# Second product of the seven-product blocks in 256-column matmuls, with shifted stationary operands

## The chip, the cores and the metric

The kernel runs on one core of a Trainium2 chip. The metric is the device time of one execution in microseconds; three runs of a kernel give a median. Each kernel also has one profiled execution, whose trace gives the start and the length of the instructions of each engine: TensorE (PE, with its loads of the stationary operand in a row of their own, PEld), VectorE (DVE), ScalarE (ACT), GpSimd (POOL) and SyncE (SP).

## What is computed

Attention with a memory term over 4 x 8 heads of 576 positions and 64 dimensions, and then two expert layers without biases over 2304 tokens of 512 features with 2048 inner features. Only the expert layers matter here:

```python
def _moe_ref(x, w_in, w_out):
    h = x @ w_in
    g = h * np.cos(h)
    return (g @ w_out).astype(np.float32)

def _moe2_ref(x, w_in, w_out):
    h = x @ w_in
    r = np.maximum(h, 0.0)
    g = r * r
    return (g @ w_out).astype(np.float32)

x = attention(q, k, v, M_prev, z_prev, beta)      # to rows of tokens x 512
return _moe2_ref(_moe_ref(x, w_in, w_out), w2_in, w2_out)
```

## The kernel before

Tokens go through an expert layer in blocks of 512, 512, 512, 256 and 512 (`CFG["sizes"]`), and the 2048 inner features in 16 feature tiles of 128. A *step* s is one feature tile f of one block j in layer p (`steps[s] = (p, j, f)`). For each step TensorE makes the first product h (128 inner features x the block's tokens), the other engines make the activation g from it, and TensorE makes the second product, which adds up over the 16 feature tiles in PSUM.

Products are to be as exact as float32, from operands in the type float32r. So each operand is kept as a high part and a rest (h and l at the end of its name: `winh`, `winl`, `wouth`, `woutl`, `gh`, `gl`), and a product is three matmuls: high x high, high x rest, rest x high. `g_f` (line 373) makes gh on ScalarE and `g_g` (line 379) gl on VectorE or GpSimd. Both take a tile of 128 x 512 from the pool `g3`, which keeps two buffers for each of the two names (line 332).

The second product is `l2` (line 880). In layer 1 the stationary operand is a 128 x 128 piece of wout and the moving one is g. In layer 2 it is the other way around: the stationary operand is a 128 x 128 piece of g, the moving one is all 512 columns of wout, and the result is 128 tokens x 512 outputs, one bank of PSUM (`acc[c]`). `evac` (line 919) copies these banks to SBUF after the last feature tile and starts their way out.

Layer 2 has two ways of making the first product. Its narrow block (256 tokens, `order2`) makes it directly, as layer 1 does (`l1`, line 310). The other four blocks (`CFG["seven"]`, steps from NS = 80 on) use Strassen's scheme with seven products for two feature tiles at a time: `product(k, i)` (line 1168) makes product i of pair k as six matmuls of 256 columns, and `combine` (line 1185) puts the products together on ScalarE and VectorE. The loop over k (line 1239) writes out the order of the work: between the seven products of pair k it puts the second product of the two steps before, in pieces (`l2(s0 - 2)` whole, `l2(s0 - 1)` in two halves of its four output tiles). There are 32 pairs, and so 64 such steps of four output tiles.

Moving operands of 256 columns don't begin at the start of their tile but 48 elements further: `span` (line 307) for the narrow block, `xpart` (line 1119) for the seven products. All others begin at the start.

Of the kernel before, what the change touches and what calls it, by code (L numbers as in the profile page):

```python
# [10 lines left out]
F32R = mybir.dt.float32r  # L11
# [116 lines left out]
def kernel(  # L128
# [39 lines left out]
    pe, act, dve, pool, sync = nc.tensor, nc.scalar, nc.vector, nc.gpsimd, nc.sync  # L168
# [125 lines left out]
    steps = [(p, j, f) for p, j, a, e in segs for f in range(a, e)]  # L294
    NS = len(steps)
    segs7 = [(2, j, 0, NF) for j in CFG["seven"]]
    steps += [(p, j, f) for p, j, a, e in segs7 for f in range(a, e)]
    opens = {(p, j, a) for p, j, a, e in segs + segs7}
    closes = {(p, j, e - 1) for p, j, a, e in segs + segs7}
# [7 lines left out]
    def span(n):  # L307
        return slice(48, 48 + n) if n == 256 else slice(0, n)
# [23 lines left out]
    g_3 = ctx.enter_context(tc.tile_pool(name="g3", bufs=2))  # L332
# [36 lines left out]
    def g_e(s):  # L369
        if steps[s][0] == 1:  # L370
            dve.tensor_tensor(out=rs[s], in0=hs[s], in1=rs[s], op=ALU.mult)

    def g_f(s):
        n = blocks[steps[s][1]][1]
        gh = g_3.tile([128, 512], F32R, tag="gh", name="gh")[:, span(n) if steps[s][0] == 1 else slice(0, n)]
        act.activation(out=gh, in_=rs[s], func=AF.Copy)
        gs[s] = gh

    def g_g(s):
        n = blocks[steps[s][1]][1]  # L380
        gl = g_3.tile([128, 512], F32R, tag="gl", name="gl")[:, span(n) if steps[s][0] == 1 else slice(0, n)]
        eng = pool if s < CFG["glp"] else dve
        eng.tensor_tensor(out=gl, in0=rs[s], in1=gs[s].bitcast(F32), op=ALU.subtract)
        gs[s] = (gs[s], gl)

    chain, made = {"a": g_a, "b": g_b, "c": g_c, "d": g_d, "s": g_s, "e": g_e, "f": g_f, "g": g_g}, set()

    def g_do(x, s):
# [487 lines left out]
    def moe(ctx, g_o, early):  # L876
        ps_a = ctx.enter_context(tc.tile_pool(name="psa", bufs=1, space=PSUM))
        acc, part = {}, {}

        def l2(s, span_=(0, 1)):  # L880
            p, j, f = steps[s]
            n = blocks[j][1]
            hi, lo = wt[p, "out", f]
            gh, gl = gs[s]
            na = KD if p == 1 else n // 128
            for c in range(int(span_[0] * na), int(span_[1] * na)):
                if (p, j, f) in opens:
                    acc[c] = ps_a.tile([128, 512], F32, tag=f"a{c}", name=f"a{c}")
                cs = slice(c * 128, (c + 1) * 128)
                if p == 1:  # L890
                    o = acc[c][:, 0:n]
                    ops = ((hi[:, cs], gh), (hi[:, cs], gl), (lo[:, cs], gh))
                else:
                    o = acc[c]
                    ops = ((gh[:, cs], hi), (gl[:, cs], hi), (gh[:, cs], lo))
                for x, (lt, rt) in enumerate(ops):
                    pe.matmul(
                        out=o, lhsT=lt, rhs=rt,
                        start=((p, j, f) in opens and x == 0),
                        stop=((p, j, f) in closes and x == 2),  # L900
                    )

        def evac_tile(c, s=0):
            if c < 2:
# [78 lines left out]
        def step(name, u, s):  # L983
# [4 lines left out]
            elif name == "L2":  # L988
                if live:
                    l2(u)  # L990
                    l2_done.add(u)
# [247 lines left out]
        for k in range(K):  # L1239
# [28 lines left out]
            if kb == (6 if k < KP else 2) and nx is not None:  # L1268
                for x in ("t1", "t2", "t3"):
                    t_make(nx, x)  # L1270
            l2(s0 - 2)
            if last:
                for x in ("b11", "b21", "t3"):
# [11 lines left out]
            if last:  # L1285
                for x in ("t2", "t4"):
                    x_h(nx, x)
                    x_l(nx, x)
            l2(s0 - 1, (0, .5 if k < K - 1 else .25))
            evac(s0 - 1, (0, .5))  # L1290
            product(k, 5)
# [94 lines left out]
```

## Time and profile before

| | us |
|---|---|
| median of 3 runs | 967.05 (966.15 to 967.24) |
| the profiled execution | 965.75 |
| its span, from the first to the last instruction | 964.0 |
| TensorE busy in the span | 956.0 (99%) |
| VectorE | 663.7 (69%) |
| ScalarE | 568.5 (59%) |

The median is read for the time, and the span for where it goes. The rest of the profiled execution's time, 1.75 us, lies around the span. A matmul's length in the trace reaches into those after it, as they are pipelined; the distance from one start to the next is what one costs when nothing waits. The lines of the trace nearly all show L48, which is the helper that hands out the instructions, so the groups are told apart by the names of their tiles: `a` is the second product's bank, `h` the first product's, `out<-moving,stationary` in either order of names.

### The profile page before, as it was taken

How to read it: one execution, taken by the hardware profiler on the slowest of the kernel's cores; microseconds unless marked ns; L12 is line 12 of the kernel's file. 1: busy time of each engine (PE TensorE's matmuls, PEld its weight loads, DVE VectorE, ACT ScalarE, POOL GpSimd, SP SyncE). 2: the span in 40 equal slices, each digit the busy share in tenths (PEclk: the TensorE clock that was granted, in tenths of full speed). 3: DMA queues.
4: the chain of work that ended last, by engine and by line, in shares of the span. 5: the costliest groups of instructions: out<-in, count | busy, mean ns of one | idle time of the engine just before them, and what ended most of it. 6: DMA issues, size and time to landing. Idle time of an engine off the chain costs nothing.

```text
span 964.0 us, 16498 instructions
## 1 busy us (share of the span) xinstructions
PE 956.0 (99%) x6030; PEld 811.4 (84%) x6030; DVE 663.7 (69%) x1381; ACT 568.5 (59%) x1235; POOL 214.3 (22%) x295
## 2 busy tenths in 40 slices
PE   8999999999999999999999999999999999999998
PEld 5777777788888888888988888999999999999997
DVE  7988888588989766687788986665654455445433
ACT  7999998777777655665777784443432232233222
POOL 7777876301111000010010002242201001000000
PEclk9999999999999999999999999999999999999999
DMA  6355654452433434243454655343441314223221
GB/s 201 125 168 182 207 208 154 150 165 65 133 97 122 136 110 149 76 142 119 134 172 141 210 167 175 111 156 128 143 152 68 99 66 154 99 66 110 91 73 44
DMA packets 69139, 126.91 MB, mean 132 GB/s; under 512 B 7106, under 2 KB 32194, under 8 KB 69058
## 3 DMA queue, kind: packets, MB, share of 16 engines
q1 hardware_dynamic: 68624, 125.44, 39.8%
q8 instruction: 47, 0.77, 0.3%
q10 hardware_dynamic: 434, 0.43, 0.1%
q14 instruction: 34, 0.28, 0.1%
HBM read 93.86 MB, written 31.98 MB: 131 GB/s over the span
## 4 chain that ended last, share of the span: by engine, by line
PE 86%; DVE 6%; ACT 3%; DMA 2%; issue 2%; SPq 0%; POOL 0%; DVEq 0%; POOLq 0%; ACTq 0%
PE a L48 35%; PE h L48 34%; PE o L48 6%; PE sps L48 5%; PE ptps L48 5%; DVE gf L48 2%; PE qps L48 2%; DVE wa L48 1%; ACT gh L48 1%; DMA wf<-ws2out 1%; DVE wb L48 1%; ACT gf L48 1%; DVE woutl L48 0%; DMA wraw<-in_moe_w_out_dram 0%; DMA qk<-in_qk_dram 0%
## 5 line engine op out<-in xcount | busy, mean ns | idle before, releaser
L48 PE MATMUL h<-xb,winh 128*128 128x256 f32 (+1 forms) x1216 | 289.7, 325 | 0.2 <-DVE gf L48 0.2
L48 PEld LDWEIGHTS h<-xb,winh 128*128 128x128 f32 x1216 | 206.9, 188 | 22.9 <-DVE gf L48 0.4
L48 PE MATMUL h<-xb,winl 128*128 128x256 f32 (+1 forms) x640 | 207.8, 325 | 0.0
L48 PEld LDWEIGHTS h<-xb,winl 128*128 128x128 f32 x640 | 121.7, 190 | 10.0
L48 PE MATMUL a<-gl,wouth 128*128 128x512 f32 (+1 forms) x320 | 118.0, 369 | 0.3 <-DVE gl L48 0.2
L48 PE MATMUL a<-gh,woutl 128*128 128x512 f32 (+1 forms) x320 | 117.6, 367 | 0.0
L48 PE MATMUL a<-gh,wouth 128*128 128x512 f32 (+1 forms) x319 | 117.3, 368 | 0.0
L48 POOL TENSOR_SCALAR wa<-wa 128x512 f32<-128x512 f32 x63 | 39.6, 629 | 343.7 <-ACT wa L48 318.2
L48 PE MATMUL a<-wouth,gl 128*128 128x512 f32 x288 | 112.5, 391 | 0.6 <-DVE gl L48 0.6
L48 PE MATMUL a<-woutl,gh 128*128 128x512 f32 x288 | 112.2, 390 | 0.0
L48 PE MATMUL a<-wouth,gh 128*128 128x512 f32 x288 | 112.2, 390 | 0.0
L48 DVE TENSOR_TENSOR hb<-h,p 128x256 f32<-128x256 f32 x64 | 27.2, 425 | 117.3 <-PE h L48 117.3
L48 POOL TENSOR_SCALAR P<-P,sm 128x384 f32<-128x384 f32 (+3 forms) x128 | 86.4, 691 | 29.3 <-ACT x L48 20.2
L48 PE MATMUL h<-xb,r 128*128 128x256 f32 x576 | 83.7, 282 | 0.0
L48 DVE TENSOR_TENSOR gf<-h,gf 128x512 f32<-128x512 f32 (+1 forms) x80 | 50.7, 634 | 47.9 <-ACT ki L48 41.2
L48 PEld LDWEIGHTS h<-xb,r 128*128 128x128 f32 x576 | 79.2, 189 | 5.3 <-DVE hb L48 0.5
L48 ACT ACTIVATE ki<-h 128x512 int32<-128x512 f32 (+1 forms) x80 | 44.1, 552 | 65.2 <-PE h L48 64.9
L48 ACT ACTIVATE gh<-hb 128x512 fp32r<-128x512 f32 x32 | 20.2, 632 | 92.6 <-DVE hb L48 92.6
L48 ACT ACTIVATE P<-P,mx 128x384 f32<-128x384 f32 (+3 forms) x128 | 70.5, 562 | 2.2 <-DVE mx L45 2.2
L48 ACT ACTIVATE gh<-gf 128x512 fp32r<-128x512 f32 (+1 forms) x96 | 53.4, 556 | 29.2 <-DVE gf L48 28.9
L48 PEld LDWEIGHTS a<-gl,wouth 128*128 128x128 f32 x320 | 60.1, 188 | 10.8 <-DVE gl L48 0.8
L48 PEld LDWEIGHTS a<-gh,woutl 128*128 128x128 f32 x320 | 60.2, 188 | 10.0
(122 smaller groups left out, 1793.5 us busy)
## 6 DMA issues: line engine op xcount, KB each, us to landing
wraw<-in_moe_w_in_dram SPq DMA_DIRECT2D x32, 512.0 KB, 4.0
wraw<-in_moe_w_out_dram SPq DMA_DIRECT2D x32, 512.0 KB, 3.9
r<-sw SPq DMA_DIRECT2D x24, 512.0 KB, 3.5
qk<-in_qk_dram SPq DMA_DIRECT2D x15, 640.0 KB, 5.2
wf<-ws2in SPq DMA_DIRECT2D x32, 256.0 KB, 2.7
r<-sw SPq DMA_DIRECT2D x24, 256.0 KB, 3.7
vr<-in_vrow_dram SPq DMA_DIRECT2D x16, 320.0 KB, 5.3
xT<-x SPq DMA_DIRECT2D x16, 288.0 KB, 2.3
```

The source lines that it names most:

```text
L48: made = call(*args, **kwargs)
```

## The change

In the steps of the seven-product blocks `l2` makes each of its three matmuls on an output tile as two, of columns 0 to 255 and 256 to 511 of wout and of the bank, with the same stationary operand. Only the first half's first matmul opens the bank. The tiles of gh and gl become 528 elements wide, in all steps, and in the steps of the seven-product blocks g stands in elements 16 to 527 of its tile, 64 bytes further than before. In all other steps g stands where it stood within its tile.

```diff
+    def part(s, n):
+        if steps[s][0] == 1:
+            return span(n)
+        return slice(0, n) if s < NS else slice(16, 16 + n)
+
     def g_f(s):
         n = blocks[steps[s][1]][1]
-        gh = g_3.tile([128, 512], F32R, tag="gh", name="gh")[:, span(n) if steps[s][0] == 1 else slice(0, n)]
+        gh = g_3.tile([128, 528], F32R, tag="gh", name="gh")[:, part(s, n)]
         act.activation(out=gh, in_=rs[s], func=AF.Copy)
         gs[s] = gh

     def g_g(s):
         n = blocks[steps[s][1]][1]
-        gl = g_3.tile([128, 512], F32R, tag="gl", name="gl")[:, span(n) if steps[s][0] == 1 else slice(0, n)]
+        gl = g_3.tile([128, 528], F32R, tag="gl", name="gl")[:, part(s, n)]
         eng = pool if s < CFG["glp"] else dve
         eng.tensor_tensor(out=gl, in0=rs[s], in1=gs[s].bitcast(F32), op=ALU.subtract)
         gs[s] = (gs[s], gl)
...
                 else:
                     o = acc[c]
                     ops = ((gh[:, cs], hi), (gl[:, cs], hi), (gh[:, cs], lo))
+                halves = (slice(0, 256), slice(256, 512)) if p == 2 and s >= NS else (slice(None),)
                 for x, (lt, rt) in enumerate(ops):
-                    pe.matmul(
-                        out=o, lhsT=lt, rhs=rt,
-                        start=((p, j, f) in opens and x == 0),
-                        stop=((p, j, f) in closes and x == 2),
-                    )
+                    for hc in halves:
+                        pe.matmul(
+                            out=o[:, hc], lhsT=lt, rhs=rt[:, hc],
+                            start=((p, j, f) in opens and x == 0 and hc.start in (0, None)),
+                            stop=((p, j, f) in closes and x == 2),
+                            skip_group_check=len(halves) > 1,
+                        )
```

## Rows read from the trace of the kernel before

**Rows 1.** The page: busy us, share of the span and instructions, by engine.

```profile
PE 956.0 (99%) x6030; PEld 811.4 (84%) x6030; DVE 663.7 (69%) x1381; ACT 568.5 (59%) x1235; POOL 214.3 (22%) x295
```

**Rows 2.** The page: the chain that ended last, shares by engine and line.

```profile
PE 86%; DVE 6%; ACT 3%; DMA 2%; issue 2%; SPq 0%; POOL 0%; DVEq 0%; POOLq 0%; ACTq 0%
PE a L48 35%; PE h L48 34%; PE o L48 6%; PE sps L48 5%; PE ptps L48 5%; DVE gf L48 2%; PE qps L48 2%; DVE wa L48 1%; ACT gh L48 1%; DMA wf<-ws2out 1%; DVE wb L48 1%; ACT gf L48 1%; DVE woutl L48 0%; DMA wraw<-in_moe_w_out_dram 0%; DMA qk<-in_qk_dram 0%
```

**Rows 3.** Timeline, 631.3 to 634.3: start, length, engine, instruction, count, idle before.

```profile
631.39 0.77 PEld L48 LDWEIGHTS h<-xb,r 128*128 128x128 f32 x6 [0.26 <-DVE hb L48]
631.39 0.97 PE L48 MATMUL h<-xb,r 128*128 128x256 f32 x6
...
632.20 0.39 PE L48 MATMUL h<-xb,winh 128*128 128x256 f32 x2
...
634.24 0.39 PE L48 MATMUL a<-wouth,gh 128*128 128x512 f32 x1
```

**Rows 4.** Timeline of the end: TensorE's last matmul and the copy behind it.

```profile
960.02 0.39 PE L48 MATMUL a<-woutl,gh 128*128 128x512 f32 x1
960.45 0.76 DVE L48 COPY ob<-a 128x256 f32<-128x256 f32 x2 [2.05 <-PE a L48]
```

**Rows 5.** Stretch 634.0 to 960.5: length, engines' busy us, clock, DMA share, GB/s.

```profile
634.00:960.50 326.50, 326.18 (x2056) 295.39 (x2054) 157.99 (x267) 102.92 (x234) 34.55 (x34) 1.00 0.30 102
```

**Rows 6.** TensorE's waits from 635 to the end: us, times, longest.

```profile
PE a L48 <- DVE gl L48: 0.2, 1, 0.2
```

**Rows 7.** TensorE's groups and one load group from 634.2: count, busy, mean ns, idle.

```profile
L48 PE MATMUL a<-wouth,gl 128*128 128x512 f32 x256 | 99.9, 390 | 0.2 <-DVE gl L48 0.2
L48 PE MATMUL a<-woutl,gh 128*128 128x512 f32 x256 | 99.8, 390 | 0.0
L48 PE MATMUL a<-wouth,gh 128*128 128x512 f32 x256 | 99.7, 390 | 0.0
L48 PE MATMUL h<-xb,winh 128*128 128x256 f32 x488 | 90.4, 282 | 0.0
L48 PE MATMUL h<-xb,r 128*128 128x256 f32 x554 | 80.5, 282 | 0.0
L48 PE MATMUL h<-xb,winl 128*128 128x256 f32 x244 | 68.7, 282 | 0.0
...
L48 PEld LDWEIGHTS a<-woutl,gh 128*128 128x128 f32 x256 | 48.1, 188 | 9.9
```

**Rows 8.** The page's costliest groups: matmuls and loads of one operand pair.

```profile
L48 PE MATMUL h<-xb,winh 128*128 128x256 f32 (+1 forms) x1216 | 289.7, 325 | 0.2 <-DVE gf L48 0.2
L48 PEld LDWEIGHTS h<-xb,winh 128*128 128x128 f32 x1216 | 206.9, 188 | 22.9 <-DVE gf L48 0.4
```

**Rows 9.** Timeline of TensorE in the last stage: twelve wide matmuls, twelve narrow ones.

```profile
644.64 0.39 PE L48 MATMUL a<-wouth,gh 128*128 128x512 f32 x1
...
647.36 0.87 PE L48 MATMUL h<-xb,r 128*128 128x256 f32 x6
...
648.77 0.39 PE L48 MATMUL a<-wouth,gh 128*128 128x512 f32 x1
```

**Rows 10.** Timeline of TensorE in layer 1's narrow block, 256 columns throughout.

```profile
464.02 0.38 PE L48 MATMUL a<-gl,wouth 128*128 128x256 f32 x1
464.24 0.29 PE L48 MATMUL a<-gh,woutl 128*128 128x256 f32 x1
...
465.46 0.50 PE L48 MATMUL h<-xb,winh 128*128 128x256 f32 x2
...
466.98 0.28 PE L48 MATMUL a<-gh,wouth 128*128 128x256 f32 x1
...
475.46 0.28 PE L48 MATMUL a<-gh,wouth 128*128 128x256 f32 x1
...
478.40 0.28 PE L48 MATMUL a<-gh,wouth 128*128 128x256 f32 x1
...
486.56 0.28 PE L48 MATMUL a<-gh,wouth 128*128 128x256 f32 x1
```

## The prediction

> **What bounds the kernel now.** I read the busy table first: TensorE works 99% of the span, VectorE 69%, ScalarE 59% [rows 1]. That share alone proves little, so I read the chain of waits next: 86% of it is TensorE, and the two matrix products of the expert layers make up 69% [rows 2]. The change touches the last stage, in which the seven-product blocks run. Its first second-product matmul starts at 634.24 [rows 3] and its last matmul at 960.02 [rows 4]. In that window VectorE is busy for 158.0 and ScalarE for 102.9 of 326.5 us [rows 5], and the list of TensorE's waits holds a single one, 0.2 us, on the way to the last block [rows 6]. So here the time is the number of matmuls times the distance from one start to the next, and nothing else ends later. The granted clock is 1.00 throughout [rows 5], the upper of its two levels. What the change is worth is therefore read from starts, and not from the durations of single matmuls (390 and 282 ns, [rows 7]), which overlap.
>
> **What the change replaces.** In the list of groups the second product of the stage has 256 matmuls for each of three operand pairs, 768 in all, each of 512 columns [rows 7]. Each becomes two of 256 columns, so 1536. A half does not do without its load of the stationary operand, although the half before it has used the same one: today (winh, xh) and (winh, xl) also follow each other with one stationary operand, and the trace still has a load for each matmul, 1216 for 1216 [rows 8]. Columns, sums, evacuations, DMAs and waits stay as they are.
>
> **The price of a start.** Twelve 512-column matmuls of the second product lie between 644.64 and 647.36: 2.72 us, 226.7 ns each. The twelve 256-column ones of two products that follow end at 648.77: 1.41 us, 117.5 ns each [rows 9]. Longer trains of 256 columns stand in the first expert layer's narrow block, where both products use that width, 24 matmuls for each feature tile. They show **two speeds**. From 466.98 to 475.46 three feature tiles, 72 matmuls, take 8.48 us: 117.8 ns each. From 478.40 to 486.56 the same number takes 8.16 us: 113.3 ns each [rows 10]. Same shapes, same buffers: 113.3 is half of 226.7, so at the quick speed a column costs what it costs in a wide matmul (0.443 ns), and at the slow one each narrow matmul carries 4.5 ns more. Nothing in the trace runs a 256-column matmul of this data type below 113.3 for longer than the rounding of single starts.
>
> The sum at the slow speed: 2 x 117.8 - 226.7 = 8.9 ns for each of the 768, **+6.8 us**. At the quick speed it is 2 x 113.3 - 226.7 = 0. There is no cover for either, as TensorE is what ends last. I take the slow speed, because it is the one that this stage shows, between these very matmuls [rows 9].
>
> The Trainium skill (TensorE: Matmul & The Clock Gate, Back-to-back issue gap) gives the warm distance as N/2.4 + 2.5 ns, estimated 215.8 for 512 columns and 109.2 for 256. This case's rows differ from both (226.7 and 113.3 or 117.8, [rows 9, 10]), and the measurement decides. By this page of the Trainium skill a pair of halves would cost 2.5 ns, an estimated +1.9 us in all; rows put its per-matmul constant at 0 or 8.9 ns, depending on the speed.
>
> **The 64 bytes.** In the program built of the kernel before, every tile that a matmul reads here begins at the same place modulo 128 bytes; the moving operands of all 256-column matmuls begin 48 elements (192 bytes) further. So moving and stationary operand stand 64 bytes apart (modulo 128) in every 256-column matmul, and 0 apart in every 512-column one. The change wants the first relation for its halves and moves the stationary operand, gh or gl, by 16 elements. But the tiles are packed: gh's two buffers now lie 2048 bytes apart, and the wider tile of 528 elements is 2112 bytes long, which is 16.5 x 128. The second buffer of each pair is thus another 64 bytes further. With the shift, even steps stand 64 apart as wanted; odd steps are back at 0. Half of the halves, 768, run in a relation that no 256-column row shows. Their bounds: below, 113.3 each (the wide matmuls at relation 0 lose nothing against it), which is -3.5 us on the sum; above, a whole load that does not run beside a matmul, as after the break that ends at 464.02, where the next start comes 0.22 us later [rows 10], about +80 us. The nearest row is the difference between the two speeds, as both look like reads that do or don't get in each other's way: another 4.5 ns, +3.5 us. For the middle I take 117.8 for these too.
>
> The packing moves things outside the stage as well. In the first layer gh and gl are the moving operands, and half of the 768 wide matmuls there (those of the second buffers) change their relation: 0 to 384 x 4.5 ns = +1.7 us. They cannot gain, as 0.443 ns a column is the lowest that the rows show. I take 0: in a wide matmul the next load's record (188 ns, [rows 7]) fits into 226.7 with room. Of the narrow block's second product 96 matmuls get a new relation, 0 to +0.4 us; I take 0. Tiles allocated behind these move by 256 bytes, which leaves all relations as they are: 0. The two ends of the last output tile now finish one half apart, which could let its first copy begin 0.1 us sooner [rows 4]: 0.
>
> **Sum.** The profiled execution took 965.75 us (span 964.0 and 1.75 around it); with +6.8 it takes 972.6. The median of the runs shown, 967.05, is 1.3 above it, so the forecast for the median is **973.9 us**.
>
> **Rivals.**
> *A, the forecast:* slow speed, the odd steps no worse. 973.9, with 971 to 977 for its own range.
> *B, the quick speed spreads; faster.* A speed holds until something breaks the train: in the narrow block the quick one begins after a stall and lasts [rows 10]. It stands right before the wide matmuls of the last stage, after a load that came late at 631.39: from 632.20 to 634.24 eighteen matmuls take 2.04 us, 113.3 each [rows 3]. Then the wide matmuls come, and what follows them is slow again [rows 9]. After the change there are no wide matmuls from 634.24 on. If the quick speed goes through the halves, all the products keep it: 1286 product matmuls in the window (488 + 554 + 244, [rows 7]) save 4.5 ns each, 5.8 us, and the halves cost 0: 961.3. Against it: the halves change the relation of the operands every few matmuls, half of the time to one that no row shows at this speed, and a stall can also end in the slow speed (465.46 to 466.98, [rows 10]). It decides the sign if the quick speed holds over more than about 55% of the matmuls.
> *C, neutral.* Only the halves are quick, or the speeds alternate: 965 to 969. The rule of the Trainium skill named above (TensorE: Matmul & The Clock Gate) would land at the upper edge of this case.
> *D, the odd steps pay.* At another 4.5 ns on 768 halves 977.4; at twice that, and with the 1.7 us of the first layer, 982.5.
> *E, the shift does nothing,* because loads and moving reads don't meet at all. Then A or C, by the speed. The Trainium skill (SBUF — State Buffer, Who interferes with whom) says this: TensorE's two read ports are independent and it never waits for anyone. Two speeds at equal addresses don't contradict it, but don't come from it either.
>
> **How the numbers follow.** A 0.37, B 0.22, C 0.18, D 0.23; E lies in A and C. A measurement of this kernel tells about 0.2% (1.9 us) from no change. Slower takes A, D and a little of C: 0.62. Same takes most of C: 0.16. Faster is B: 0.22. The range reaches from B's value to beyond D's first one, 960.5 to 980.5; a B that also quickens the tail and a D at double price, together about 0.15, stay outside. Cases of both signs carry weight, so A's own range, 971 to 977, stands beside it.
>
> **What would show it.** The changed kernel must have 1536 matmuls of 256 columns under the second product in the last stage, each with a load, and still no waits. Twelve halves by 0.118 us or by 0.113 tell A from C. Two products, now 1.41 us [rows 9], at 1.36 would show B. Halves at 0.118 in even steps and more in odd ones would show D, and a wide second-product matmul of the first layer above 0.227 its side cost. The prediction is wrong if halves start less than 113 ns apart, if the odd steps are the quicker ones, or if a wait grows in the stage.

## The result and the profile after

The changed kernel takes 975.47 us (median of 4 runs, 974.86 to 977.34), against 966.6 us (965.1 to 967.24) for the kernel before in the same comparison: a ratio of 1.0097, with an interval of 1.0082 to 1.0112. It is slower by 8.9 us. The profiled execution took 977.34 us, with a span of 975.6.

The page of the changed kernel, first its busy us, share of the span and instructions by engine, then the chain that ended last:

```profile
PE 967.1 (99%) x6798; PEld 848.1 (87%) x6798; DVE 665.0 (68%) x1381; ACT 568.7 (58%) x1235; POOL 214.8 (22%) x295
PE 91%; DVE 4%; ACT 2%; DMA 1%; issue 1%; SPq 0%; DVEq 0%; POOL 0%; ACTq 0%; POOLq 0%
```

TensorE has 768 matmuls more than before (6798 against 6030, [rows 1]) and as many more loads: every half has its own. TensorE's busy time grew by 11.1 us and the span by 11.6; the other engines have what they had, within 1.3 us. The last stage still has one wait, the same as before [rows 6], and the full clock. The changed kernel's last stage in the views of [rows 5] and [rows 6]:

```profile
640.50:972.30 331.80, 331.29 (x2815) 330.87 (x2813) 157.86 (x266) 102.69 (x233) 33.61 (x33) 1.00 0.30 101
...
PE a L48 <- DVE gl L48: 0.2, 1, 0.2
```

So the time is again a number of matmuls times the distance from one start to the next. Start distances by stretch, from the first start of a stretch to that of the next one, in the profiled executions (us):

| stretch | before | after | difference |
|---|---|---|---|
| up to layer 1 (attention) | 174.97 | 176.18 | +1.2 |
| layer 1, its three first wide blocks | 267.72 | 269.62 | +1.9 |
| layer 1's narrow and last wide block, start of layer 2 | 143.57 | 144.94 | +1.4 |
| up to the last stage | 47.98 | 48.92 | +0.9 |
| last stage, first to last second-product start | 325.78 | 332.04 | +6.3 |
| behind it, to the end of the execution | 5.73 | 5.64 | -0.1 |

Two of these rows came out alike when the changed kernel ran once more (experiment 11): 269.65 and 332.03. The others were 175.57, 144.15 and 48.52 there, so most of the 1.2 us ahead of layer 1 and part of the rest belong to this one execution, which is 1.9 us above its median.

Inside the last stage the two kinds of steps differ: the even ones, whose 24 halves run in one train (`l2(s0 - 2)`), and the odd ones, whose halves run in two trains of 12. Timeline of TensorE in the changed kernel (start, length, instruction, count of matmuls in the line), from one pair of steps to the next:

```profile
700.32 0.87 PE L48 MATMUL h<-xb,r 128*128 128x256 f32 x6
...
703.15 0.40 PE L48 MATMUL a<-wouth,gh 128*128 128x256 f32 x2
...
704.56 0.39 PE L48 MATMUL a<-wouth,gh 128*128 128x256 f32 x2
...
705.92 0.87 PE L48 MATMUL h<-xb,r 128*128 128x256 f32 x6
...
707.34 0.40 PE L48 MATMUL a<-wouth,gh 128*128 128x256 f32 x2
...
708.77 0.40 PE L48 MATMUL h<-xb,winh 128*128 128x256 f32 x2
```

Four products, 24 matmuls, take 703.15 - 700.32 = 2.83 us, 117.9 ns each. The 24 halves of the even step take 2.77 us, 115.4 each: the first twelve 1.41 us (117.5 each) and the last twelve 1.36 (113.3 each). Two products take 1.42, 118.3 each, and the first 12 halves of the odd step 1.43, 119.2 each. Over all steps but those of the last block's tail, which have no products between them, the halves of an even step take 115.6 ns in the mean (114.3 in the first one), those of an odd step 119.2 (from 118.7 to 119.7 for the single trains of 12), and all halves together 117.4. The products take 117.9, against 117.8 before.

In layer 1 the wide second product got slower too. Timeline of TensorE in the changed kernel, twelve wide matmuls of an odd and twelve of an even step:

```profile
311.50 0.40 PE L48 MATMUL a<-gh,wouth 128*128 128x512 f32 x1
...
314.28 0.61 PE L48 MATMUL h<-xb,winh 128*128 128x512 f32 x2
...
317.00 0.39 PE L48 MATMUL a<-gh,wouth 128*128 128x512 f32 x1
317.22 0.40 PE L48 MATMUL a<-gl,wouth 128*128 128x512 f32 x1
317.46 0.39 PE L48 MATMUL a<-gh,woutl 128*128 128x512 f32 x1
...
319.74 0.62 PE L48 MATMUL h<-xb,winh 128*128 128x512 f32 x2
```

They take 2.78 and 2.74 us, 231.7 and 228.3 ns each (over all such steps the medians are 231.2 and 228.9), against 226.7 for a wide matmul before [rows 9]. In the even step only the matmul on gl is late: 0.24 us from its start to the next.

### The profile page after: what moved, and what is told of

The parts are those of the page before. It is cut to its first block, busy times and chain, and to the rows that moved or that the text cites. A ratio compares the mean times of both kernels' runs of the same rounds, so it can differ in the third digit from the quotient of the medians.

```text
span 975.6 us, 18037 instructions
## 1 busy us (share of the span) xinstructions
PE 967.1 (99%) x6798; PEld 848.1 (87%) x6798; DVE 665.0 (68%) x1381; ACT 568.7 (58%) x1235; POOL 214.8 (22%) x295
## 4 chain that ended last, share of the span: by engine, by line
PE 91%; DVE 4%; ACT 2%; DMA 1%; issue 1%; SPq 0%; DVEq 0%; POOL 0%; ACTq 0%; POOLq 0%
PE a L48 37%; PE h L48 35%; PE o L48 6%; PE sps L48 5%; PE ptps L48 5%; PE qps L48 2%; DVE gf L48 1%; DMA wf<-ws2out 1%; DVE wa L48 1%; ACT gh L48 1%; DVE gl L48 1%; DVE wb L48 0%; DMA wraw<-in_moe_w_out_dram 0%; ACT gf L48 0%; DVE P L48 0%
## 5 line engine op out<-in xcount | busy, mean ns | idle before, releaser
L48 PE MATMUL a<-gl,wouth 128*128 128x512 f32 (+1 forms) x320 | 119.1, 372 | 0.2 <-DVE gl L48 0.2
L48 PE MATMUL a<-gh,wouth 128*128 128x512 f32 (+1 forms) x319 | 118.3, 371 | 0.4 <-ACT gh L48 0.4
L48 PE MATMUL a<-wouth,gl 128*128 128x256 f32 (+1 forms) x544 | 115.2, 288 | 1.1 <-DVE gl L48 1.0
L48 PE MATMUL a<-wouth,gh 128*128 128x256 f32 (+1 forms) x544 | 114.5, 287 | 0.0
L48 PE MATMUL a<-woutl,gh 128*128 128x256 f32 (+1 forms) x544 | 114.3, 287 | 0.0
L48 PEld LDWEIGHTS a<-wouth,gl 128*128 128x128 f32 x544 | 84.1, 188 | 2.6 <-DVE gl L48 1.9
L48 PEld LDWEIGHTS a<-woutl,gh 128*128 128x128 f32 x544 | 84.9, 189 | 1.3
L48 PEld LDWEIGHTS a<-wouth,gh 128*128 128x128 f32 x544 | 84.4, 189 | 0.6
L48 PEld LDWEIGHTS h<-xb,r 128*128 128x128 f32 x576 | 74.5, 189 | 0.4 <-DVE hb L48 0.2
```

The source lines that it names most:

```text
L48: made = call(*args, **kwargs)
```

## The experiments

Two words are used throughout. The *difference* of a matmul is the address at which its moving operand begins minus that of its stationary operand, modulo 256 bytes. The *speed* of a 256-column matmul is quick (113.3 ns from start to start) or slow (117.8), as in [rows 10]. In the changed kernel the halves have differences of 192 (gh) and 64 (gl) in even steps, and 128 and 0 in odd ones; the products have 192.

The theories at first were: **theory 1**, the difference sets the price, and odd steps are slow because theirs is a multiple of 128; **theory 2**, the order of the work sets it (an even step's halves are one train of 24, an odd step's two of 12). Later, theory 1 was split: **1a**, each difference has its price; **1b**, what counts is that all narrow matmuls, products and halves, begin at the same pair of addresses modulo 256, so that a train that is once quick isn't thrown out of its speed.

**1. The wanted difference in every step.** gh and gl become pieces of one tile, 512 elements apart, so that nothing is packed at 2112 bytes; layer 1 stays as it was before.

```diff
+    gq = g_3.tile([128, 2112], F32R, name="gq", bufs=1)
...
-        gh = g_3.tile([128, 528], F32R, tag="gh", name="gh")[:, part(s, n)]
+        gh = gq[:, 512 * (s % 2):512 * (s % 2) + 528][:, part(s, n)]
...
-        gl = g_3.tile([128, 528], F32R, tag="gl", name="gl")[:, part(s, n)]
+        gl = gq[:, 1024 + 512 * (s % 2):1024 + 512 * (s % 2) + 528][:, part(s, n)]
```

> As the changed kernel, but the four buffers of gh and gl lie 2048 bytes apart again (pieces of one tile of 2112 elements), so that the shift by 64 bytes gives the wanted relation in every step and nothing changes before the seven-product blocks. Theory 1 (the relation of moving and stationary operand sets the price): odd steps become as quick as even ones are in the changed kernel, 115.8 ns a half instead of 119.6, and the 3 us or so that layer 1 and the narrow block lose go away: halves cost 2 x 115.8 - 226.7 = 4.9 ns a pair, +3.8 us, 970.4 where the kernel before takes 966.6. Theory 2 (the order of work does it: even steps run as a train of 24 halves... of 24 matmuls, odd ones in two of 12): odd steps stay at 119.6, +6.7 us, 973.3.

Measured: 969.51 us against 966.5, a ratio of 1.003 (1.0018 to 1.0043). Timeline of TensorE in its last stage, columns as above:

```profile
706.10 0.86 PE L48 MATMUL h<-xb,r 128*128 128x256 f32 x6
...
708.85 0.63 PE L48 MATMUL a<-wouth,gq 128*128 128x256 f32 x4
...
711.43 0.40 PE L48 MATMUL a<-woutl,gq 128*128 128x256 f32 x2
```

The time is close to theory 1, but not by its mechanism. The halves run at 117.5 to 117.8 ns in every step (here 22 of them in 2.58 us, 117.3), the odd ones no better than the forecast's slow speed. What gained are the products: 24 in 2.75 us, 114.6, most of them at 113, and 115.0 in the mean of the stage. So theory 1 is right that even and odd steps become alike, theory 2 falls, and a third thing showed: what follows a train of halves need not keep its speed.

**2. Halves without the shift,** in the tiles of before (difference 0 in all steps).

```diff
-        return slice(0, n) if s < NS else slice(16, 16 + n)
+        return slice(0, n)
...
-        gh = g_3.tile([128, 528], F32R, tag="gh", name="gh")[:, part(s, n)]
+        gh = g_3.tile([128, 512], F32R, tag="gh", name="gh")[:, part(s, n)]
```

(gl likewise.)

> The halves alone: tiles of 512 elements as before, no shift, so every half stands 0 bytes (modulo 128) from its stationary operand, and layer 1 is as before. Theory 1: all halves at the price of the odd steps of the changed kernel, 119.6 ns, +9.6 us, 976.2; and the product matmuls unchanged at 117.8. Theory 2: even steps stay at 115.8 and odd ones at 119.6, +6.7 us, 973.3.

Measured: 971.73 us, a ratio of 1.0058 (1.0043 to 1.0073). Both theories expected more. Timeline of TensorE:

```profile
706.82 0.86 PE L48 MATMUL h<-xb,r 128*128 128x256 f32 x6
...
709.56 0.39 PE L48 MATMUL a<-wouth,gh 128*128 128x256 f32 x2
...
712.18 0.40 PE L48 MATMUL a<-woutl,gh 128*128 128x256 f32 x2
```

The 22 halves between the last two lines take 2.62 us, 119.1 each, close to the odd steps of the changed kernel. Every such train begins with quicker ones and settles at 120.0 ns from the eleventh on: difference 0 costs 2.2 ns beyond the slow speed once it has settled, and 1.0 in the mean of all halves (118.8). But the 24 products before them take 2.74 us, 114.2. In this run and in experiment 1, where the halves of all steps have one difference, the products are quick, which neither theory had.

**3. The shift without the halves:** tiles of 528 elements and the 64 bytes, second product in wide matmuls.

```diff
-                halves = (slice(0, 256), slice(256, 512)) if p == 2 and s >= NS else (slice(None),)
+                halves = (slice(None),)
```

> The wider tiles and the shift of the changed kernel, but the second product in matmuls of 512 columns as before. Theory 1: layer 1 and the narrow block cost what they cost in the changed kernel, about +3 us, and the 768 wide matmuls of the last stage cost some 4.5 ns more each, as the wide ones of layer 1 do in the new relations (229 to 235 ns against 226.6): +3.5 us, in all 973. Theory 2, by which the addresses are free: 966.6.

Measured: 973.32 us, a ratio of 1.0072 (1.0057 to 1.0087), as theory 1 expected. The wide matmuls of the last stage now lie 231.1 ns apart in even steps and 230.3 and 232.3 in the two trains of an odd one, instead of 226.7. In the timeline of TensorE eleven of an even step take 2.54 us, 230.9 each:

```profile
701.12 0.39 PE L48 MATMUL a<-wouth,gh 128*128 128x512 f32 x1
...
703.66 0.39 PE L48 MATMUL a<-woutl,gh 128*128 128x512 f32 x1
```

So the shift and the packing alone cost most of what the whole change costs (6.8 of 8.9 us), and a wide matmul pays for its operands' addresses too. Layer 1's three blocks take 269.76 us here, as in the changed kernel.

**4. The halves one after the other** instead of in turn.

```diff
-                for x, (lt, rt) in enumerate(ops):
-                    for hc in halves:
+                for hc in halves:
+                    for x, (lt, rt) in enumerate(ops):
```

> As the changed kernel, but not in turn: the three matmuls on the first half of an output tile, then the three on the second, so that each matmul adds to the columns of the one before it. Theory 1: same operands, same relations, within 1.5 us of the changed kernel's 975.5. Rival theory 3 (taking the halves in turn spares a matmul from waiting for the sum of the one before, which is what makes half of the even steps quick): even steps go to 118 or more, +1.7 us and up, 977 or more.

Measured: 973.53 us, a ratio of 1.0075 (1.006 to 1.009), 1 to 2 us less than the changed kernel, where no difference or a loss was expected. Even steps run at 114.5 and odd ones at 118.1 ns in the mean, each 1.1 below the changed kernel's. Taking the halves in turn therefore saves nothing.

**5. One pair of addresses for all narrow matmuls of layer 2.** The tiles of wout get pools of their own, 192 bytes further than those of win, and g stands at the start of its piece in the last stage. So halves and products read from the same pair of addresses modulo 256. Layer 1's operands move along.

```diff
+    wAo = ctx.enter_context(tc.tile_pool(name="wAo", bufs=1))
...
+    wpool = {"in": [wA] * NF, "out": [wAo] * NF}
...
+        x = 0 if s >= NS else 96 if steps[s][0] == 1 and n == 256 else 48
+        return slice(x, x + n)
```

> The halves with one pair of start addresses for the whole last stage. The tiles of wout lie 192 bytes further than those of win (in a run of their own, behind a gap), gh and gl follow them before the seven-product blocks, and in these blocks they lie where win lies: so the halves read their moving operand from 64 and their stationary one from 128 (modulo 256), exactly as the products do (in the first experiment the halves read from 128 and 192, the same distance at other places). All wide matmuls keep distance 0. Theory 1b (a train of narrow matmuls keeps its phase, and start address and phase together decide between 113.3 and 117.8 ns, so that it is the change of addresses between halves and products that turns one of the two slow): both run at one speed throughout; quick, that is 2 x 113.3 - 226.7 = 0 for the halves and -4.5 ns on some 1340 product matmuls, -6 us, 960.5; or, if the train's entry sets it slow, 117.8 everywhere, +6.8 us, 973.3; nothing between. Rival 1a (the distance alone decides, and the rest is chance): as the first experiment, 969.5, with one role quick and the other slow.

Measured: ten executions in two groups, seven from 963.6 to 965.6 and three from 972.8 to 977.8; a ratio of 1.0007 (0.997 to 1.0043). In the profiled one, which is of the first group, the last stage takes 320.28 us, with halves and products at 113.3 throughout. Theory 1a (969.5) falls. Two groups fit 1b, by which the whole stage has one speed, the quick or the slow one. That the stage was slow throughout in the second group is not shown, as none of it was profiled and its times spread over 5 us; what picks the group was not found. The first group lies 3 to 5 us above the 960.5 that 1b gave, and layer 1 accounts for 2.4 of them in the profiled execution: its three first blocks take 270.14 us in this layout, instead of 267.72. Timeline of TensorE there:

```profile
313.85 0.62 PE L48 MATMUL h<-xb,winh 128*128 128x512 f32 x2
...
316.61 0.62 PE L48 MATMUL a<-gq,wouth 128*128 128x512 f32 x2
```

Both products have difference 0 in this layer, but no longer the same addresses: the first reads both operands from 128 (modulo 256), the second both from 64. The twelve wide matmuls of the first product take 2.76 us, 230 each, although nothing of theirs has moved. The medians by place in the train, over all of layer 1's wide trains, show where: the second product's matmuls are late in the first three places (229, 233 and 231 ns) and then back at 227, the first product's in most of the first ten. So a wide matmul's time depends not on its own difference alone, but also on the addresses of the train before it.

**6. The same layout, second product wide.**

```diff
-                halves = (slice(0, 256), slice(256, 512)) if p == 2 and s >= NS else (slice(None),)
+                halves = (slice(None),)
```

> The addresses of e5_one_offset with the wide second product of the kernel before. All distances between moving and stationary operand are those of the kernel before. Theory 1b and 1a: no change, 966.5 within 1 us; products slow, as they are entered from wide matmuls. If the layout itself costs or gives something, it shows here.

Measured: 968.84 us, a ratio of 1.0024 (1.0014 to 1.0035), more than expected, for two reasons. Layer 1's three blocks cost 2.5 us more, as in experiment 5. And the premise on the distances was wrong for the last stage: its wide matmuls have difference 192 in this layout, not 0. Timeline of TensorE there:

```profile
750.06 0.85 PE L48 MATMUL h<-xb,r 128*128 128x256 f32 x6
...
752.78 0.62 PE L48 MATMUL a<-wouth,gq 128*128 128x512 f32 x2
...
755.58 0.85 PE L48 MATMUL h<-xb,r 128*128 128x256 f32 x6
```

The 24 products take 2.72 us, 113.3 each, and the twelve wide matmuls 2.80, 233.3 each (232.7 in the mean of the stage). The products are quick in all of the stage, the wide matmuls 6 ns dearer: gain and loss nearly cancel (325.05 us, against 325.78 before).

**7. The products at difference 0,** in the kernel before.

```diff
-            return xb[:, 48 + 512 * (2 * slot[x] + lo):48 + 512 * (2 * slot[x] + lo + 1)]
+            return xb[:, 512 * (2 * slot[x] + lo):512 * (2 * slot[x] + lo + 1)]
```

> The kernel before with one change: the moving operands of the seven products begin at the start of their tiles instead of 48 elements further, so that their 1344 matmuls stand 0 bytes (modulo 128) from their stationary operands, as the halves without the shift do. Theory 1: 120 ns a start, as those halves, instead of 117.8: +3.0 us, 969.5. A theory by which the place of operands does not matter: 966.5.

Measured: 971.34 us, a ratio of 1.0052 (1.0035 to 1.0068). Timeline of TensorE, 24 products and the wide matmuls behind them:

```profile
705.96 0.88 PE L48 MATMUL h<-xb,r 128*128 128x256 f32 x6
...
708.83 0.40 PE L48 MATMUL a<-wouth,gh 128*128 128x512 f32 x1
...
710.22 0.39 PE L48 MATMUL a<-wouth,gh 128*128 128x512 f32 x1
...
711.58 0.88 PE L48 MATMUL h<-xb,r 128*128 128x256 f32 x6
```

The products take 2.87 us, 119.6 each instead of 117.8, and settle at 120.0 as the halves of experiment 2 do. That is the price of difference 0 again, on matmuls that the change doesn't touch. The wide matmuls, whose own addresses are as before, rose as well, which was not expected: to 229.0 ns in even and 231.3 in odd steps. Here the first six of a train take 1.39 us (231.7 each) and the last six 1.36 (226.7 each), and so it is in every even step. The price of a wide matmul therefore hangs not on its own difference alone, but also on what runs before it, and what it pays for that ends after six matmuls.

**8. One pair of addresses in layer 2 alone.** As experiment 5, but layer 1 keeps the addresses of the kernel before: the pieces of wout lie in one run per pool, and only layer 2 writes and reads them 192 bytes further. In the narrow block of layer 2 g stands 48 elements further, in the last stage at the start of its tile of 512.

```diff
+    def w_out_at(phase, f, l):
+        t, r = (wo["A"], NA - 1 - f) if f < NA else (wo["B"], NF - 1 - f)
+        x = 2 * DM * r + DM * l + (48 if phase == 2 else 0)
+        return t[:, x:x + DM]
...
+            hi = w_out_at(phase, f, 0)
...
+        return slice(48, 48 + n) if s < NS else slice(0, n)
```

> As e5_one_offset, but only layer 2's wout lies 192 bytes further (in one run of tiles for each pool, f descending, so that the shifted tile covers none that layer 1 still needs); layer 1 has the addresses of the kernel before. Theory 1b: layer 1's wide matmuls go back from 231 to 227 ns, 2.4 us less than e5, and the last stage runs at one speed throughout: 961.5 where it is entered quick, and 973.5 where it is entered slow, with a few executions of each kind, as in e5 (7 quick and 3 not). Rival (e5's gain came from its layout and not from one pair of addresses): no execution under 964.

Measured: **960.79 us** against 966.11, a ratio of 0.9942 (0.9929 to 0.9954): faster than both kernels, and its five executions lie within 0.7 us. Timeline of TensorE and, for its last stage, the stretch in the columns of [rows 5]:

```profile
703.17 0.84 PE L48 MATMUL h<-xb,r 128*128 128x256 f32 x6
...
705.89 0.39 PE L48 MATMUL a<-woB,gh 128*128 128x256 f32 x2
...
708.38 0.39 PE L48 MATMUL a<-woB,gh 128*128 128x256 f32 x2
...
635.00:955.50 320.50, 319.99 (x2817) 319.55 (x2816) 156.50 (x267) 102.85 (x233) 33.75 (x33) 1.00 0.31 105
```

24 products take 2.72 us and the 22 halves behind them 2.49, 113.3 and 113.2 each. The stage takes 320.35 us from its first to its last start, 5.4 less than before, with the same work in halves. Layer 1's three blocks are back at 267.77. The rival falls: all five executions lie under 964. None lies near 973.5, where a few were expected.

**9. Experiment 8 with one wide tile left:** the first output tile of each even step stays wide.

```diff
-                halves = (slice(0, 256), slice(256, 512)) if p == 2 and s >= NS else (slice(None),)
+                halves = (slice(0, 256), slice(256, 512)) if p == 2 and s >= NS and (c or s % 2) else (slice(None),)
...
```

> As e8_layer2_offset, but the first output tile of every second step keeps its three matmuls of 512 columns (96 wide matmuls instead of 192 halves). Theory 1b: in e6_one_offset_wide every train of narrow matmuls after wide ones at these addresses was quick, so the wide tile puts the train back to the quick speed every 10 us, whatever stalls came before. It costs 96 times (232 - 226.7) ns, 0.5 us: 962, and no slow executions. If wide matmuls don't set the speed, the spread of e8 stays.

Measured: 967.26 us, a ratio of 1.001 (1.0001 to 1.0019): a miss. Three wide matmuls in every pair of steps take the whole gain. Timeline of TensorE:

```profile
705.47 0.87 PE L48 MATMUL h<-xb,r 128*128 128x256 f32 x6
...
708.29 0.39 PE L48 MATMUL a<-woB,gh 128*128 128x512 f32 x1
...
711.03 0.84 PE L48 MATMUL h<-xb,r 128*128 128x256 f32 x6
...
712.39 0.39 PE L48 MATMUL a<-woB,gh 128*128 128x256 f32 x2
...
715.79 0.84 PE L48 MATMUL h<-xb,r 128*128 128x256 f32 x6
...
718.51 0.39 PE L48 MATMUL a<-woA,gh 128*128 128x512 f32 x1
...
721.33 0.87 PE L48 MATMUL h<-xb,r 128*128 128x256 f32 x6
...
722.74 0.40 PE L48 MATMUL a<-woA,gh 128*128 128x256 f32 x2
```

Before the wide tile 24 products take 2.82 us, 117.5 each; after it and nine pairs of halves 12 products take 1.36, 113.3. In the next pair of steps it is the other way around, 113.3 before the wide tile and 117.5 after it, and so it goes on, pair by pair, up to the last block's tail: each wide tile turns one speed into the other. So 1b's expectation, that a train falls into the quick speed and stays there, is too simple. Addresses alone don't set the speed: the wide matmuls here read from the same pair of addresses as the narrow ones, and still change it.

**10. The last stage of the change, and nothing else.** Halves at exactly the addresses of the changed kernel, everything ahead of the last stage as before.

```diff
+        return slice(0, n) if s < NS else slice(16 + 16 * b, 16 + 16 * b + n)
...
+        gh = gq[:, 512 * (s % 2):][:, part(s, n, s % 2)]
```

> The changed kernel's last stage alone: halves, and gh and gl at the places modulo 256 that the changed kernel gives them there; before the seven-product blocks they lie as in the kernel before. The wider tiles' cost before that stage (layer 1's and the narrow block's matmuls at new distances: +1.9 us between 177 and 446 us, and some 1 to 2 us up to 640, in the traces) is gone. If the traces are read rightly, the last stage's +6.3 us stay and 966.5 + 6.3 = 972.8 results, 2 to 3 us less than the changed kernel beside it. If the difference between the two traces ahead of the last stage is chance, it is as long as the changed kernel.

Measured: 972.88 us against 966.39, a ratio of 1.0066 (1.0053 to 1.0079), as expected: the last stage alone costs 6.5 us. It takes 332.00 us, and layer 1's three blocks 267.89.

**11. The changed kernel again,** beside experiment 10 on the same chip.

> The changed kernel once more, beside the run above on the same chip: 975 to 975.5.

Measured: 974.67 us, a ratio of 1.0087 (1.0073 to 1.0101). The difference to experiment 10, 1.8 us by the medians, is what the packing costs outside the last stage; by the profiled executions it is 2.8, of which 1.8 lie in layer 1's three first blocks and 0.7 in the stretch that holds its last one.

## Why the prediction was right, and where it was not

The forecast was 973.9 us by slow halves in a stage without cover, and 975.5 came out. It started from a median of 967.05 for the kernel before, and in the comparison that kernel took 966.6; so +6.8 us stand against +8.9.

*Bound and counts:* right. One wait of 0.2 us as before, clock 1.00, 768 matmuls and 768 loads more, and the stage's length is the sum of its start distances.

*The price of a half:* right in size. The forecast took 117.8 ns for each half and +6.8 us; measured are 117.4 as the mean, +6.3 us in the profile and +6.5 us where only this stage was changed (experiment 10). Its make-up was wrong: the equal price for even and odd steps is the mean of two errors, and that they cancel is luck. Even steps turn quick in their middle (115.6 as a mean), odd steps pay (119.2). The nearest row named for the odd steps, another 4.5 ns, would have been too much: they pay 1.4 ns beyond the slow speed, and a train at difference 0 alone pays 2.2 once it has settled (experiments 2 and 7).

*The side cost in layer 1, taken as 0:* this step failed. The reason given, that a load's record of 188 ns fits into 226.7 with room, says nothing on the price of a difference. Wide matmuls pay as well: 228.3 and 231.7 ns in even and odd steps, a mean of 3.3 ns above 226.7. On the 576 matmuls of the three first blocks that makes 1.9 us, the 1.9 of the table; on all 768 it makes 2.5, beyond the bound of 1.7. The bound was too low because it counted differences modulo 128 and so only the second buffers, half of the 768: the first buffer of gl, 128 bytes off, pays too (the 0.24 us in the even step above), which makes it two thirds. With the 1.9 us put in, the forecast would have been +8.7.

*Rival B* (the quick speed spreads) fell in the changed kernel, at the place and for the reason named against it. Its timeline at the start of the last stage:

```profile
639.66 0.39 PE L48 MATMUL a<-wouth,gh 128*128 128x256 f32 x2
...
642.40 0.87 PE L48 MATMUL h<-xb,r 128*128 128x256 f32 x6
...
643.82 0.40 PE L48 MATMUL a<-wouth,gh 128*128 128x256 f32 x2
```

The first 24 halves are quick (2.74 us, 114.2 each), and the 12 products behind them are slow again (1.42, 118.3), although no wide matmul stands between. A quick speed that goes through halves and products exists, though, and its price was right: 5.8 us less than before was forecast, and with one pair of addresses for products and halves the kernel takes 5.3 less (experiment 8). *Rival C* fell. *Rival D* was right in kind, with about a third of its price in the stage (1.4 of 4.5 ns), and the layer 1 part that was put into its upper end is what came. *Rival E*, that the shift does nothing, falls with experiments 3 and 7, in which nothing but addresses moved and the time rose by 0.5 to 0.7%. That it is loads and moving reads that meet is not shown by this: the runs show only that the addresses matter. The Trainium skill says that TensorE's two read ports are independent and that it never waits for anyone (SBUF — State Buffer, Who interferes with whom); by that alone addresses would cost nothing here, and the start distances of this kernel, 226.7 to 233 ns for one shape by its addresses and those before it, show that they do.

*Still open:* what the two speeds are. The runs show that a train can go from one to the other within a few matmuls (in the even steps of the change it does so in its middle, in the same pattern of addresses), that differing start addresses or a different width between can turn them, and that experiment 5's times fell into two groups while experiment 8's five executions all lie by 961. With three times of ten in experiment 5's upper group, five in a row in the lower would come by chance about one time in six, so whether experiment 8 has an upper group too they don't show, nor what decides at the start. Only one pair of addresses (64 and 128) was tried for all narrow matmuls.

## What to carry to other kernels

Where TensorE never waits, price a change of matmul shape by the distance from start to start in long trains, and look for more than one value of it there: the same 2,820 narrow matmuls of one stage took 320 us in one layout and 332 in another. A tile made wider for a shift moves the second buffer and every other user of the pool, so work out the start addresses of all of them. In this kernel the split paid only where all narrow matmuls of the stage kept one pair of start addresses modulo 256 bytes, with none of another width between (experiment 8, and seven of ten executions of experiment 5). Of the other layouts none gained. So measure the layout together with the split.

## What was not expected of the hardware

A wide matmul's start distance depends on where its operands begin. In a settled train it is 226.7 ns where both begin at the same place modulo 256. Wide trains with other differences have means of 228 to 233. Even at difference 0 the first few matmuls of a train pay when the train before it reads from other addresses (227.7 and 230.2 as means in experiment 5's layer 1) or is a narrow one with difference 0 (229 to 231 in experiment 7). A narrow one has 113.3 or 117.8 at one and the same pair of addresses, and settles at 120.0 at difference 0. So the widths want opposite things here: at difference 0 the wide matmuls were at their cheapest and the narrow ones at their dearest, and at 192 a wide one took 232.7 (experiment 6). And three wide matmuls among 84 narrow ones were enough to turn the speed of all that followed until the next three, back and forth. With about 0.5 us for the wide ones themselves that makes up the 6.5 us between experiments 8 and 9.
